# Products of Wv and M by heads, in 32-column tiles of TensorE

## Chip, cores and metric

The kernel runs on one core of a Trainium2 chip. The metric is the device time of one execution in microseconds (us), the median of several runs.

## The reference

A block with adaptive layer norm: linear attention, then a gated feed-forward network, on x of 2048 rows by 1024 columns. Cut to what matters here:

```
mod = silu(c) @ w_mod                       # six rows of 1024: sa, ca, ga, sb, cb, gb
h   = layernorm(x) * (1 + ca) + sa
q, k, v = split(h @ wqkv)                   # 32 heads of 32
pq, pk  = phi(q), phi(k)                    # phi(t) = (t + 1 if t > 0 else exp(t)) + 1e-6
kv  = einsum('bhsd,bhse->bhde', pk, v)      # per head, 32 x 32
z   = sum over s of pk                      # per head, 32
o   = (pq @ kv) / (pq @ z + 1e-6)
x   = x + ga * (o @ wo)
x   = x + gb * ((gelu(h2 @ w_gate) * (h2 @ w_up)) @ w_down),  h2 from layernorm(x), cb, sb
```

The inputs are bf16.

## The kernel before

v itself is never formed. For each group g of four heads (128 columns, `NG` = 8 groups) the kernel computes M = pk^T h, 128 x 1024 (`m_tile`, with a column of ones that gives z), transposes it with a DMA (`m_t`, the tile `MTB`, two buffers used in turn, g % 2), and multiplies it with the group's columns of Wv (`kv_prod`): kv = M Wv, summed over 1024 in 8 steps of 128 (`dc`). In `kv_prod` one matmul per step makes a full 128 x 128 product of all four heads with all four heads; the blocks that belong to one head lie on the diagonal, and VectorE takes out two 64 x 64 pieces, multiplies them by a block mask (`BMASK`) and writes them to `KVT` (L920).

After that `w2_pair(i)` multiplies kv of groups 2i and 2i + 1 with rows of wo (W2 = kv wo, in 64 x 64 tiles of the array, L1203), scaled before by ga (`wofold`, L1214); `den` makes the denominators (L1246) and `mod_rows` the modulation rows (L840), both in 32-column tiles; `wo_mm` multiplies pq with W2 (L1292).

The order on TensorE is written by hand: a loop over 24 tiles (g, k) of `m_tile`, three for each group, and a table `HOOK` that says what follows tile n. Tile n accumulates in PSUM bank n % 4 and ScalarE copies it out (`mcp`, L900). Before the change `kv_prod` always uses bank 4; `w2_pair` uses banks 4 to 7, `den` 3 and 5, the modulation rows behind tile 16 bank 2. Groups 5, 6 and 7 come behind the last tile and between the first `wo_mm`. SP's queue issues the transposes and loads in program order too.

For VectorE, ScalarE and GpSimd the order inside this stretch is not the program's but that of a planner (`Sched.reorder`): it runs through the operations with estimated costs and, whenever an engine is free, takes among the operations that are ready by then the one with the earliest due time. The costs are a table in us per operation, by engine and kind; for TensorE it has

```
"m": (0.145, 0.15), "kv": (0.056, 0.15), "den": (0.027, 0.15), "modr": (0.04, 0.15)
```

and the table applies to each matmul. VectorE's sums over weights of the modulation (L796, L798, L816, L819: `acc`, `gacc`) have no part in the attention and fill its time; the row `gbr` of the table and `modp` read them.

Of the kernel before, what the change touches and what calls it, by code (L numbers as in the profile page):

```python
# [8 lines left out]
ALU = mybir.AluOpType  # L9

P = 128
# [6 lines left out]
NDC = D // P  # L18
NG = 8
HPG = 4  # L20
# [310 lines left out]
def bass_adaLN_cond__linear_attn_block__geglu_ffn__prompt_kernel(  # L331
# [18 lines left out]
    with ExitStack() as es:  # L350
# [3 lines left out]
        ps_all = es.enter_context(nc.psum_tensor("ps_all", [P, 8 * 512], f32))  # L354
        ps16 = ps_all.bitcast(bf16)

        def at(name, shape, dty, off):
            return nc.alloc_sbuf_tensor_at(name, shape, dty, offset=ABASE + off, align_bytes=4)
# [20 lines left out]
        WV = at("wv", [P, NG, NDC, P], bf16, OFF_WK)  # L379
# [12 lines left out]
        MTB = [at(f"mtb{i}", [P, NDC, P], bf16, OFF_MTB[i]) for i in range(2)]  # L392
# [21 lines left out]
        KVT = at("kvt", [P, NG, P], bf16, OFF_KVT)  # L414
# [22 lines left out]
        IDENT, BMASK, BM32, Z32 = (_small[k] for k in ("ident", "bmask", "bm32", "z32"))  # L437
# [7 lines left out]
        def r_sm(name):  # L445
            return [(SMO[name], SMO[name] + SMSZ[name], name)]
# [27 lines left out]
        def r_mtb(i):  # L474
            return [(OFF_MTB[i], OFF_MTB[i] + 2048, f"mtb{i}")]

        def r_wv(g):
            return [(OFF_WK + g * 2048, OFF_WK + (g + 1) * 2048, "wv")]
# [61 lines left out]
        def r_kvt(g0, g1):  # L540
            return [(OFF_KVT + g0 * 256, OFF_KVT + g1 * 256, "kvt")]

        def pr(b):
            return [(b * 2048, (b + 1) * 2048)]

        def PS(b, c0=0, c1=512):
            return ps_all[:, b * 512 + c0: b * 512 + c1]
# [4 lines left out]
        sch = Sched()  # L552
        T, A, V, G, Q = PE_, ACT_, DVE_, POOL_, SP_
# [12 lines left out]
        def pset_writer(b, o):  # L566
            for t_ in pr(b):
                sch.ps.set_writer(t_[0], t_[1], o)
# [49 lines left out]
        for q in range(1, 4):  # L618
            wmq_dma(q)
            for d0, d1 in ((2 * q, 2 * q + 1), (2 * q + 1, 2 * q + 2)):  # L620
# [8 lines left out]
               rd=r_sm("c8") + r_sm("ident"), pwr=pr(4))  # L629
# [4 lines left out]
               rd=r_sm("thc") + r_sm("chalf"), wr=r_sm("siluT"))  # L634
# [173 lines left out]
        def gb_rows():  # L808
            mod_rows(((0, 2, 6, lambda j, h: (HLG[:, j, h, :], r_hlg(j, h))),))
            o_gb[0] = mod_store(2, 6, MRG, [(OFF_TMP + 4096, OFF_TMP + 5120, "mrg")], 2)  # L810
# [94 lines left out]
        def m_t(g):  # L905
            i = g % 2
            tdma(Q, MTB[i][:, :, :], MB[g][:, :], r_mb(g), r_mtb(i), f"mT{g}")

        def kv_prod(g, bank):
            i = g % 2  # L910
            o = None
            for dc in range(NDC):
                o = sch.op(T, lambda e, dc=dc: e.matmul(PS(bank, 0, P), WV[:, g, dc, :], MTB[i][:, dc, :],  # L913
                                                        start=(dc == 0), stop=(dc == NDC - 1)),
                           rd=r_wv(g) + r_mtb(i), pwr=(pr(bank) if dc == 0 else ()), note=f"kv g{g} dc{dc}")
            pset_writer(bank, o)
            z = 64 * (g % 2)
            for h in range(2):
                a, gz = 64 * h, g // 2 * 2 + h
                sch.op(V, lambda e, a=a, gz=gz: e.tensor_tensor(KVT[z:z + 64, gz, 0:64], ps_all[a:a + 64, bank * 512 + a:bank * 512 + a + 64], BMASK[a:a + 64, a:a + 64], ALU.mult),  # L920
                       prd=pr(bank), rd=r_sm("bmask"), wr=r_kvt(gz, gz + 1), note=f"kvt{g}", overwrite_ok=True)

        bank_i = [0, 4]
# [137 lines left out]
        def nbank():  # L1061
            b = ROT[bi[0] % 8]
            bi[0] += 1
            return b
# [6 lines left out]
        def wofold(*kcs):  # L1071
            for kc in kcs:
                rg = r_wo(kc)
                sch.op(V, lambda e, kc=kc: e.tensor_tensor(WO[:, kc, :], WO[:, kc, :], GAB[:, :], ALU.mult),
                       rd=rg + R_GAB, wr=rg, note=f"wofold {kc}")
# [92 lines left out]
        def ga_pass():  # L1168
            b = 6
            mod_rows(((0, 2, b, hl_src),))  # L1170
            o_r = mod_store(2, b, MROW0, [(XHO[2], XHO[2] + 1024, "mrow0")], 0)
            row_load(GAB, R_GAB, 0, 0, "gab", o_r)
# [6 lines left out]
        for n, (kind, a_, b_) in enumerate(seq):  # L1179
            bank = nbank()  # L1180
# [11 lines left out]
        def z32():  # L1192
            sch.op(V, lambda e: e.tensor_tensor(Z32[:], BM32[:], ZCOLS[:, :].unsqueeze(2).to_broadcast([P, NG, NH]), ALU.mult),
                   rd=r_sm("bm32") + r_sm("zcols"), wr=r_sm("z32"), note="z32")
# [32 lines left out]
        def mod_pass():  # L1227
            assert mdone[0] >= 48 and not late
            mod_rows(((2, 4, 2, hl_src),))
            o_sc[0] = mod_store(4, 2, MROW[1], r_2k(OFF_ROW + 2048, "mrow1"), 1)  # L1230
# [3 lines left out]
        def mod_load():  # L1234
            for dst, nt, a0 in ((SBT, "sbT", 0), (CBT, "cbT", 2)):
                sch.dma(Q, lambda e, dst=dst, a0=a0: e.dma_start(dst[:, :], scr_row[1, a0:a0 + 2, :].rearrange("a (b p) -> p (a b)", p=P)),
                        wr=r_sm(nt), deps=[o_sc[0]], note=nt)
# [3 lines left out]
        def den(pr_, b):  # L1241
            o = None
            for g in range(NG):
                for i in range(4):
                    sg, t0 = 2 * pr_ + i // 2, (i % 2) * HW
                    o = sch.op(T, lambda e, g=g, i=i, sg=sg, t0=t0: e.matmul(  # L1246
                        ps_all[32 * i:32 * (i + 1), b * 512:b * 512 + HW], Z32[:, g, :], PQ[sg][:, g, t0:t0 + HW],
                        start=(g == 0), stop=(g == NG - 1)),
                        rd=r_sm("z32") + r_pq(sg, g, g + 1, t0, t0 + HW), pwr=(pr(b) if g == 0 else ()), note=f"den{pr_} {g}.{i}")
            pset_writer(b, o)  # L1250
            sch.op(V, lambda e: e.tensor_scalar(RDC[:, :], PS(b, 0, HW), 1e-6, None, op0=ALU.add), prd=pr(b), wr=r_sm("rdc"), note=f"dene{pr_}")
            sch.op(V, lambda e: e.reciprocal(RDC[:, :], RDC[:, :]), rd=r_sm("rdc"), wr=r_sm("rdc"), note=f"rden{pr_}")
            def store():
                o_rd[pr_] = sch.dma(Q, lambda e: e.dma_start(scr_rd[2 * pr_:2 * pr_ + 2].rearrange("s f k g t -> (s f k g) t"), RDC[:, :]),
                          rd=r_sm("rdc"), note=f"rden{pr_}.st")
            return store
# [30 lines left out]
        def wo_mm(c_, b0, gs):  # L1287
# [9 lines left out]
            if gs[-1] == NG - 1:  # L1297
# [10 lines left out]
        wo_load(1)  # L1308
        NWO = 5
        tiles = [(g, k) for g in range(4) for k in range(3)] + [(g, 0) for g in range(4, NG)] + [(g, k) for g in range(4, NG) for k in (1, 2)]  # L1310
        HOOK = {0: "ga", 6: "kv0", 10: "kv1", 11: "w0", 13: "kv2", 15: "kv3 z32", 16: "modp den0 w1 sbl st0", 17: "rb0.0 rb0.1", 18: "",
                19: "kv4", 20: "den1 gbr st1 ps0.0", 22: "ps0.1"}
        st = {}

        def hook_run(f):
            if f[:2] == "kv":
                kv_prod(int(f[2:]), 4)
            elif f == "ga":
                ga_pass()
            elif f == "gbr":  # L1320
                assert mdone[0] == 64
                gb_rows()
            elif f == "modp":
                mod_pass()
            elif f == "sbl":
                mod_load()
            elif f == "z32":
                z32()
            elif f[:3] == "den":
                st[int(f[3:])] = den(int(f[3:]), (3, 5)[int(f[3:])])  # L1330
            elif f[:2] == "st":
                st[int(f[2:])]()
            elif f[:2] == "ps":
                pq_scale(int(f[2]), int(f[4]), GH[0] + GH[1])
            elif f[:2] == "rb":
                rb_load(int(f[2]), (int(f[4]),))
            elif f[0] == "w":
                w2_pair(int(f[1:]))
# [6 lines left out]
        for n, (g, k) in enumerate(tiles):  # L1345
            m_tile(g, k, n % 4, n % 2)
            if n == len(tiles) - 1:
                kv_prod(5, 4)
            if k == 2:
                m_t(g)  # L1350
            if n == NWO:
                wo_load(2)
                wo_load(3)
            for _ in range(3):
                mod_step()
            if 2 <= n <= 9:
                wofold(n - 2)
            while pend and n > 1:
                wm_dma(*pend.pop(0))
            if n in (6, 7):  # L1360
                gb_load(0, n - 6)
            if n == 11:
                wt_dma(0)
                gb_load(1, 0)
                gb_load(1, 1)
            for f in HOOK.get(n, "").split():
                hook_run(f)
# [487 lines left out]
        for n in range(12):  # L1855
            q, i = divmod(n, 4)
# [6 lines left out]
        for u in range(2 * NFP):  # L1863
# [5 lines left out]
            else:  # L1869
                a = ACTS.get(u, ((), ()))  # L1870
# [143 lines left out]
```

## Time and profile before

| | us |
|---|---|
| median of 3 runs | 781.45 (780.92 to 781.78) |
| the profiled execution | 780.61 |
| its span in the profile | 778.8 |
| TensorE busy | 771.8 (99%) |
| VectorE busy | 649.1 (83%) |
| ScalarE busy | 377.2 (48%) |

The tiles of M and all products of the change lie between about 127 us and 196 us. PE is TensorE's matmuls, PEld its weight loads, DVE VectorE, ACT ScalarE, POOL GpSimd, SP the engine that issues the DMAs; L12 is line 12 of the kernel. Matmuls are pipelined: the time from the start of one to the start of the next is what one costs, and the duration that the profile gives for one is longer. In the chain of waits a row is the start, the length and what was done.

### The profile page before, as it was taken

Reading aid. Unit: us, or ns where it says so; the run is one execution under the profiler, and the core shown is the slowest. Engines: PE = TensorE matmul, PEld = TensorE weight load, DVE = VectorE, ACT = ScalarE, POOL = GpSimd, SP = SyncE. Lnnn points to the kernel's source line nnn. Section 1 sums busy time; section 2 is a strip of 40 time slices with the busy share of each in tenths; the row PEclk is TensorE's granted clock in tenths of the full one; section 3 lists DMA queues with packets and bytes.
Section 4 is the critical chain, followed back from the end, with each engine's and each line's share of the span. In section 5 each row is a group of like instructions: output and inputs, shape, how many; then the busy total and the mean of one; then the engine's idle time right before and its main releaser. Section 6 shows DMA issues by size and latency. Waiting matters only on the chain.

```text
span 778.8 us, 10822 instructions
## 1 busy us (share of the span) xinstructions
PE 771.8 (99%) x3879; PEld 498.5 (64%) x3879; DVE 649.1 (83%) x970; ACT 377.2 (48%) x635; POOL 48.8 (6%) x126
## 2 busy tenths in 40 slices
PE   7999999999999999999999999999999999999998
PEld 4444445666445667767676767677676667777776
DVE  6699989897898878787989888888989987667668
ACT  2497743242484477877755565555555221101111
POOL 2131300000331011100000000000000000000000
PEclk9999999999999999999999999999999999999999
DMA  9789749949996258967353865535356434443341
GB/s 287 254 172 249 160 93 220 258 124 206 209 274 177 82 146 205 234 172 216 100 144 108 256 205 174 145 100 162 92 153 213 138 124 126 136 148 100 130 144 54
DMA packets 196941, 130.22 MB, mean 167 GB/s; under 512 B 69517, under 2 KB 182677, under 8 KB 195865
## 3 DMA queue, kind: packets, MB, share of 16 engines
q1 hardware_dynamic: 196872, 129.55, 61.9%
q8 instruction: 30, 0.49, 0.3%
q14 instruction: 23, 0.18, 0.1%
q10 hardware_dynamic: 16, 0.00, 0.0%
HBM read 92.55 MB, written 23.35 MB: 149 GB/s over the span
## 4 chain that ended last, share of the span: by engine, by line
PE 97%; DMA 1%; SPq 1%; DVE 0%; issue 0%; DVEq 0%
PE ps_all L1472 45%; PE ps_all L1684 22%; PE ps_all L895 7%; PE ps_all L1292 7%; PE ps_all L934 7%; PE ps_all L880 7%; DMA wmq<-in_w_mod_dram 1%; PE ps_all L913 0%; PE ps_all L1607 0%; PE ps_all L766 0%; PE ps_all L1203 0%; PE ps_all L1246 0%; PE ps_all L969 0%; SPq L592 0%; SPq L603 0%; SPq L598 0%
## 5 line engine op out<-in xcount | busy, mean ns | idle before, releaser
L1472 PE MATMUL ps_all<-ss,tp 128*128 128x512 f32 x896 | 214.3, 396 | 0.0
L1472 PEld LDWEIGHTS ps_all<-ss,tp 128*128 128x128 f32 x896 | 168.2, 188 | 37.8 <-DVE ss L1427 0.3
L1684 PE MATMUL ps_all<-dt,sb 128*128 128x512 f32 x440 | 104.7, 394 | 0.0
L1472 PE MATMUL ps_all<-h2a,wt 128*128 128x512 bf16 x448 | 101.5, 380 | 0.0
L1495 ACT ACTIVATE ge<-ps_all 128x512 f32<-128x512 f32 x112 | 64.1, 596 | 73.9 <-DVE ps_all L1483 62.1
L1684 PEld LDWEIGHTS ps_all<-dt,sb 128*128 128x128 f32 x440 | 82.5, 188 | 18.5 <-issue 0.3
L1490 DVE TENSOR_TENSOR ps_all<-ps_all,es 128x512 f32<-128x512 f32 x54 | 37.6, 699 | 49.7 <-ACT es L1480 49.3
L1502 DVE TENSOR_TENSOR ys<-ge,ps_all 128x512 bf16<-128x512 f32 x112 | 74.5, 684 | 2.9
L1472 PEld LDWEIGHTS ps_all<-h2a,wt 128*128 128x128 bf16 x448 | 37.9, 98 | 57.2 <-ACT ps_all L1477 16.9
L1447 DVE TENSOR_TENSOR tp<-wt,tp 128x1024 fp32r<-128x1024 bf16 x56 | 68.2, 1218 | 0.0
L1447 DVE TENSOR_TENSOR tp<-wt 128x1024 fp32r<-128x1024 bf16 x56 | 68.1, 1217 | 0.0
L880 PE MATMUL ps_all<-wk,h1T 128*128 128x512 bf16 x248 | 56.8, 379 | 0.3 <-DVE h1T L724 0.2
L934 PE MATMUL ps_all<-h1T,wq 128*128 128x512 bf16 x256 | 56.7, 379 | 0.0
L1292 PE MATMUL ps_all<-w,pq 128*128 128x512 bf16 x256 | 56.4, 379 | 0.0
L1472 PE MATMUL ps_all<-ar,tp 128*128 128x512 f32 x224 | 55.6, 390 | 0.0
L869 ACT ACTIVATE eb<-ps_all 128x512 f32<-128x512 f32 x64 | 36.4, 593 | 37.0 <-PE ps_all L880 15.2
L1710 ACT ACTIVATE de<-ps_all 128x512 f32<-128x512 f32 x14 | 8.3, 596 | 91.3 <-PE ps_all L1684 91.3
L1684 PE MATMUL ps_all<-wd,ya 128*128 128x512 bf16 x220 | 49.2, 379 | 0.0
L1472 PEld LDWEIGHTS ps_all<-ar,tp 128*128 128x128 f32 x224 | 42.0, 188 | 8.9
L1477 ACT ACTIVATE ps_all<-ps_all 128x512 f32<-128x512 f32 x56 | 32.6, 582 | 30.9 <-PE ps_all L1472 30.9
L934 PEld LDWEIGHTS ps_all<-h1T,wq 128*128 128x128 bf16 x256 | 25.0, 98 | 29.9
L1292 PEld LDWEIGHTS ps_all<-w,pq 128*128 128x128 bf16 x256 | 24.6, 98 | 30.2 <-issue 1.1
(141 smaller groups left out, 985.3 us busy)
## 6 DMA issues: line engine op xcount, KB each, us to landing
wt<-in_B_w_gate_dram SPq DMA_DIRECT2D x28, 512.0 KB, 4.0
wt<-in_B_w_up_dram SPq DMA_DIRECT2D x28, 512.0 KB, 5.2
scr_y<-ys SPq DMA_DIRECT2D x28, 512.0 KB, 3.2
ya<-scr_y SPq DMA_DIRECT2D x14, 896.0 KB, 5.0
rb<-scr_rd SPq DMA_DIRECT2D x32, 256.0 KB, 6.0
wd<-in_B_w_down_dram SPq DMA_DIRECT2D x7, 1024.0 KB, 7.6
wmst<-in_w_mod_dram SPq DMA_DIRECT2D x6, 1024.0 KB, 5.7
wmq<-in_w_mod_dram SPq DMA_DIRECT2D x8, 512.0 KB, 6.7
```

Of the source, the lines that this page charges most:

```text
L869: sch.op(A, lambda e: e.activation(EB[i][:, :], PS(bank), ACTF.Exp), prd=pr(bank), wr=rng, note=f"{note}.exp")
L880: o = sch.op(T, lambda e, dc=dc: e.matmul(PS(bank), H1[sg][:, ci, dc, :], W_[:, dc, jg * 512:(jg + 1) * 512], start=(dc == 0), stop=(dc == ...
L895: o = sch.op(T, lambda e, c_=c_: e.matmul(PS(bank, 0, n), PK[c_][:, g * P:(g + 1) * P], xrow(c_, o_, o_ + n), start=(c_ == 0), stop=(c_ == ...
L934: o = sch.op(T, lambda e, dc=dc: e.matmul(PS(b), WQ[:, dc, qc * P:(qc + 1) * P], H1[sg][:, :, dc, :], start=(dc == 0), stop=(dc == NDC - 1 ...
L1292: last[half] = sch.op(T, lambda e, g=g, half=half: e.matmul(PS(b0 + half), PQ[sg][:, g, ci * P:(ci + 1) * P], W2[:, g, half * 512:(half + ...
L1447: sch.op(V, lambda e: e.tensor_tensor(TP[k][:], in0, in1 if k in (0, 2) else in1[:], ALU.subtract), rd=r0 + r1, wr=r_tp(k), deps=[x1_ops[7 ...
L1472: o = sch.op(T, lambda e, l_=l_, r_=r_, dc=dc: e.matmul(PS(b), l_, r_, start=fresh and dc == 0, stop=dc == ND2 - 1, skip_group_check=True) ...
L1477: sch.op(A, lambda e: e.activation(PS(BB + t), PS(BA + t), ACTF.Copy), prd=pr(BA + t), pwr=pr(BB + t), note="pcp")
L1490: sch.op(V, lambda e: e.tensor_tensor(PS(BC + t), PS(BC + t), ES[t][:, :], ALU.add), prd=pr(BC + t), rd=r_2k(OFF_ES[t], f"es{t}"), pwr=pr( ...
L1495: sch.op(A, lambda e: e.activation(GE[i][:, :], PS(b), ACTF.Gelu_apprx_tanh), prd=pr(b), wr=r_2k(OFF_GE[i], f"ge{i}"), note="gelu")
L1502: sch.op(V, lambda e: e.tensor_tensor(YS[s_][:, 2 * h:2 * h + 2, t, :], q(GE[i][:, :]), q(PS(b + 1)), ALU.mult), rd=r_2k(OFF_GE[i], f"ge{i ...
L1684: o = sch.op(T, lambda e, l_=l_, r_=r_, j=j, dst=dst: e.matmul(dst, l_[:, 0, :], r_, start=(k in (1, 5) or k == 7 and 0 < ca < 4 * CPG - 2 ...
```

## The change

`kv_prod` makes the four 32 x 32 products of the heads alone. Each step of 128 is now four matmuls, one for each head: 32 columns of Wv as weights in one column tile of the array, 32 columns of the transposed M as the moving operand, and the result in 32 partitions and 32 columns of PSUM. So all four heads lie in the same 32 columns, and the eviction reads these twice side by side under the same mask. The planner's table is not changed.

The places change too. Groups 0 and 1 are computed together behind tile 8 (before: behind tiles 6 and 10), groups 2 and 3 together behind tile 15 (before: 13 and 15), group 4 behind tile 20 straight in front of the second denominators (before: behind tile 19). Groups 5, 6 and 7 stay where they are. The banks of groups 0 to 4 are now 3, 4, 1, 2 and 3.

```diff
             for dc in range(NDC):
-                o = sch.op(T, lambda e, dc=dc: e.matmul(PS(bank, 0, P), WV[:, g, dc, :], MTB[i][:, dc, :],
-                                                        start=(dc == 0), stop=(dc == NDC - 1)),
-                           rd=r_wv(g) + r_mtb(i), pwr=(pr(bank) if dc == 0 else ()), note=f"kv g{g} dc{dc}")
+                for h in range(HPG):
+                    o = sch.op(T, lambda e, dc=dc, h=h: e.matmul(ps_all[32 * h:32 * (h + 1), bank * 512:bank * 512 + 32], WV[:, g, dc, 32 * h:32 * (h + 1)],
+                                                                 MTB[i][:, dc, 32 * h:32 * (h + 1)], start=(dc == 0), stop=(dc == NDC - 1)),
+                               rd=r_wv(g) + r_mtb(i), pwr=(pr(bank) if dc == 0 and h == 0 else ()), note=f"kv g{g} dc{dc}.{h}")
...
-                sch.op(V, lambda e, a=a, gz=gz: e.tensor_tensor(KVT[z:z + 64, gz, 0:64], ps_all[a:a + 64, bank * 512 + a:bank * 512 + a + 64], BMASK[a:a + 64, a:a + 64], ALU.mult),
+                sch.op(V, lambda e, a=a, gz=gz: e.tensor_tensor(KVT[z:z + 64, gz, 0:64].rearrange("p (k c) -> p k c", k=2),
+                       ps_all[a:a + 64, bank * 512:bank * 512 + 32].unsqueeze(1).to_broadcast([64, 2, 32]),
+                       BMASK[a:a + 64, a:a + 64].rearrange("p (k c) -> p k c", k=2), ALU.mult),
...
-        HOOK = {0: "ga", 6: "kv0", 10: "kv1", 11: "w0", 13: "kv2", 15: "kv3 z32", 16: "modp den0 w1 sbl st0", 17: "rb0.0 rb0.1", 18: "",
-                19: "kv4", 20: "den1 gbr st1 ps0.0", 22: "ps0.1"}
+        HOOK = {0: "ga", 11: "w0", 15: "kv2 kv3 z32", 16: "modp den0 w1 sbl st0", 17: "rb0.0 rb0.1", 18: "",
+                20: "kv4 den1 gbr st1 ps0.0", 22: "ps0.1"}
...
-                kv_prod(int(f[2:]), 4)
+                kv_prod(int(f[2:]), (1, 4, 1, 2, 3)[int(f[2:])])
...
+            if n == 8:
+                kv_prod(0, 3)
+                kv_prod(1, 4)
```

## The prediction

> **What bounds the kernel now.** I read the page first, then what TensorE waits for, then the chain of waits in order of time over 15 to 30 us and 120 to 200 us, where the edited lines run, then the timeline of the same stretch for the weight loads and VectorE.
>
> ```profile
> PE 771.8 (99%) x3879; PEld 498.5 (64%) x3879; DVE 649.1 (83%) x970; ACT 377.2 (48%) x635; POOL 48.8 (6%) x126
> ...
> PE 97%; DMA 1%; SPq 1%; DVE 0%; issue 0%; DVEq 0%
> ```
>
> TensorE is busy for 99% of the span and makes 97% of the chain that ended last. All its waits:
>
> ```profile
> PE ps_all L628 <- POOL bm L582: 2.5, 1, 2.5
> PE ps_all L766 <- DMA wmq<-in_w_mod_dram: 0.7, 1, 0.7
> PE ps_all L880 <- DVE h1T L724: 0.2, 1, 0.2
> ```
>
> That is 3.4 us, all in the first stages. From 126 us to 196 us it never waits, so every nanosecond that its own instructions lose or gain there moves the end, unless it runs into something that is late. The chain, with the products that change on L913 (x8 is one group, the last x16 two):
>
> ```profile
> 129.34 0.33 PE ps_all L840 x8
> 129.67 14.04 PE ps_all L895 x96
> 143.71 0.45 PE ps_all L913 x8
> 144.16 9.29 PE ps_all L895 x64
> ...
> 171.35 7.08 PE ps_all L895 x48
> ...
> 181.20 0.99 PE ps_all L1246 x32
> 182.19 0.22 PE ps_all L840 x8
> 182.41 7.08 PE ps_all L895 x48
> ...
> 193.62 0.92 PE ps_all L913 x16
> 194.53 0.86 PE ps_all L1292 x4
> 195.40 0.56 PE ps_all L1203 x8
> ```
>
> The reader is to see three prices. A product costs 0.45 us for 8 matmuls, 56 ns each. L840 and L1246 already run in 32-column tiles: two groups of four 256-wide matmuls take 0.22 us behind other such work (182.19), 0.33 us behind full-width work (129.34), so going into tiles costs 0.11 us. Coming back: 48 matmuls of L895 take 7.08 us, where 64 take 9.29 us (145 ns each, 6.97 us for 48), so 0.11 us again.
>
> The narrowest matmuls in the trace, one column against a full weight load:
>
> ```profile
> 23.78 0.38 PE ps_all L766 x16
> ```
>
> 24 ns for a load and its matmul. And loads in 32-column tiles:
>
> ```profile
> 169.31 0.12 PEld L840 LDWEIGHTS ps_all<-hl,ones 128*32 128x32 bf16 x8 [0.28 <-issue]
> ```
>
> Each lasts 92 to 96 ns in the trace's own listing of that line, and all eight are over in 0.12 us: they start within some 25 ns, and in that time four matmuls start between them. So four column tiles load and run beside each other.
>
> **The change, part by part.** Groups are those of four heads, 0 to 7. *Removed:* six times 0.45 us and once 0.92 us (rows of L913 in the chain), 3.62 us of TensorE.
>
> *Added, the products:* each of the 8 becomes 32 loads of 32 columns and 32 matmuls of 32 columns, as 8 groups of four tiles, 64 groups in all. No row shows a group that narrow. Below, streaming alone: the 256-wide group takes 0.11 us, an eighth is 14 ns. Above, the 256-wide group's 109 ns, if the loads and not the columns set it. The nearest row is L766, 24 ns: 32 columns are nearer to 1 than to 256, and the loads run side by side. I take 27 ns, a little more since eight instructions must be issued for it: 64 x 0.027 = 1.73 us.
>
> A rule of the Trainium skill speaks against the change here. Column tiling excludes Fast Weight Load (TensorEngine Tiling (Array Packing), Gotcha 2: Feature Incompatibilities), and a plain load takes its columns over 1.2 in ns (TensorE: Matmul & The Clock Gate, LDWEIGHTS): an estimate of 27 ns for 32 columns. Four in series would make 107 ns a group and the sum +4.1 us; side by side, as the loads of 169.31 start, they change nothing in it.
>
> *Added, the changes of mode:* groups 0 and 1 stand together, 2 and 3 together, 5 alone, 6 and 7 together (they stood so before), each between full-width matmuls: 4 x 0.22 = 0.88 us. Group 4 stands in front of the denominators, which paid for their way in already: nothing.
>
> *VectorE, L920:* the same 16 evictions of 64x64, now reading 32 columns twice. The trace's rows have 210 to 229 ns for one; I take no change. If the repeated read doubled it, only the last four would show: in front of 195.40 they have about 0.1 us to spare (result of group 6 at 194.12, four of 0.25 us, and the product that reads them at 195.40), and groups 6 and 7 coming 0.27 us sooner does not shift that balance, since the four matmuls of L1292 between keep their time. Price at most 0.9 us; below, nothing.
>
> *Moved:* groups 0, 2 and 4 go later and group 1 goes two tiles earlier. Group 1 needs its transposed M: the transpose is issued at 141.96 us and takes 5.6 us to land, 147.6; it is now wanted at about 148.5 us. Margin 0.9 us, cost nothing; if 2 us late it would cost 1.1 us. On SP's queue the transposes into the same two buffers wait for these products: that of g=2 is issued behind tile 8 and needs tile 8's copy anyway (0.46 us after the tile), while group 0 is over 0.3 us after it; those of g=4 and 6 come at least one tile behind their readers. So SP is held no longer. The transposes for groups 4 to 7 land 3.2 to 8.6 us after issue, partly behind the reciprocals' loads (rb), whose start hangs on the denominators and so moves forward with TensorE: group 5 gains on its transpose by 0.24 us, and I cost that at nothing, at most 0.4 us if the transfers do not move.
>
> *PSUM banks:* products used bank 4 only; now group 0 takes bank 3, 2 takes 1, 3 takes 2, 4 takes 3. New waits: tile 11 for group 0's eviction, tile 17 for group 2's, and the modulation rows behind tile 16 (bank 2) for group 3's. The last is tight, and is the second rival below.
>
> *Sum:* -3.62 + 1.73 + 0.88 = -1.01 us. The profiled execution took 780.61 us (span 778.8 and 1.8 around it), so 779.6; the median of the runs is 0.84 us above it: 780.4 us. With both ends of the group's price: -1.84 us at 14 ns, +4.2 us at 109 ns.
>
> **The rivals.**
>
> *Each matmul pays the pace, not each group (slower).* If 24 ns is the least time from one matmul to the next whatever its tile, or the rate at which TensorE is fed, a product costs 32 x 24 = 0.77 us. It decides as soon as a group costs more than 43 ns ((3.62 - 0.88) / 64). Price: 8 x 0.77 + 0.88 - 3.62 = +3.4 us, 784.9 us. For it: the denominators' 32 pairs take 0.87 us, 27 ns each, which does not contradict it, and nothing in the trace issues over some 85 instructions in a microsecond for long, where a product would now need 64 in 0.22 us. Against it: the eight loads in 25 ns. Chance 0.12. The Trainium skill (TensorEngine Tiling (Array Packing), Instruction Overhead) has such an overhead, about 60 cycles for each matmul however narrow, and advises against tiling where a dimension is already small; it does not say whether tiles pay it side by side.
>
> *The order on VectorE.* The kernel's planner writes VectorE's order from a table in which each matmul of a product costs 0.056 us. With 32 instead of 8 it believes a product takes 1.79 us; it will think TensorE some 5 us later behind group 3 than behind the same tile before, and fill VectorE with other work ahead of the evictions. Now:
>
> ```profile
> 168.02 0.48 DVE L920 TENSOR_TENSOR kvt<-ps_all,bmask 64x64 bf16<-64x64 f32 x2
> 168.53 1.23 DVE L1214 TENSOR_TENSOR wo<-wo,gab 128x1024 bf16<-128x1024 bf16 x1
> 171.15 0.42 DVE L1251 TENSOR_SCALAR rdc<-ps_all 128x256 f32<-128x256 f32 x1 [1.39 <-PE ps_all L1203]
> 171.49 0.48 DVE L796 TENSOR_SCALAR gacc<-wmg,silf 128x512 f32<-128x512 bf16 x1
> ```
>
> Group 3's eviction must be over when the rows of L840 want bank 2, at some 168.8 us by my sum; its product is ready at 166.6. If the plan puts the scaling of L1214 (1.2 us) or the first sums of L796 and L798 (0.5 and 0.7 us, on weights whose load is issued at 162.97 us and takes 3.6 to 8.2 us) ahead of it, it ends at 169.6 to 171, and TensorE waits 0.8 to 2.2 us: 781.2 to 782.6 us. Against it: VectorE stood idle for 1.06, 1.47 and 0.24 us in front of earlier evictions, which it can now fill. Chance 0.20, of which 0.05 over +1.56 us.
>
> *Cheaper than I think.* At 14 ns a group, with drains shorter because the tiles are: -1.8 us, 779.6 us. For it: streaming is all that the 256-wide groups show. Against: no pair in the trace takes less than 24 ns. Chance 0.18 for more than 1.56 us.
>
> *It does not do what it says:* tiles that do not run side by side give the first rival's time or the 109 ns end, 785.6 us, and are in its chance.
>
> **How the numbers follow.** 0.2% is 1.56 us, about what a measurement of this kernel can tell from no change. My forecast, 780.4 us, has 0.46 and lies within it; a late transpose or slower evictions (0 to +1 us) have 0.04, the order on VectorE 0.15 within and 0.05 beyond, the pace 0.12, the cheap case 0.18. Faster 0.18, same 0.65, slower 0.17. The range holds forecast and cheap case from 779.4 us, and reaches past VectorE's 2.2 us to 783.0; left out are the pace and some of the tails.
>
> **What would show it.** On the chain: L913 some 0.22 us for x32 and 0.43 us for x64; the first L895 behind each stretch 0.11 us late; group 4 and the denominators in one piece of some 1.2 us. TensorE still without waits after 126 us. Wrong if L913 shows 0.8 us for x32 (the pace), or if PE waits for kvt on L920 or for mtb.

## The result, and the profile after

The changed kernel takes 784.16 us (median of 6 runs, 783.11 to 785.54), the kernel before in the same comparison 781.49 us (6 runs, 780.57 to 781.90). The ratio is 1.0036, with the interval 1.0023 to 1.0049: slower by some 2.7 us, where I had forecast 780.4 us and at most 783.0. The profiled execution took 783.11 us with a span of 781.3 us, 2.5 us more span than before. The edits move the lines behind them: the product of L913 is now L914, the eviction L921, the denominators L1249, W2 L1206, `wo_mm` L1295.

The page of the changed kernel, the busy times and the shares of the chain that ended last:

```profile
PE 768.1 (98%) x4017; PEld 496.9 (64%) x4071; DVE 650.0 (83%) x970; ACT 377.3 (48%) x635; POOL 48.5 (6%) x126
...
PE 88%; DVE 4%; SPq 3%; DMA 3%; issue 1%; ACT 0%; DVEq 0%; ACTq 0%
```

TensorE's busy time is 3.7 us less and the kernel is longer. But most of the 3.7 us is not work saved: this trace has 4017 matmuls against 4071 weight loads, so 54 matmuls have no record. A second profile of the kernel before (experiment 0) lacks 54 as well, and shows almost the same busy time as the changed kernel:

```profile
PE 768.5 (99%) x3825; PEld 498.4 (64%) x3879; DVE 649.2 (83%) x970; ACT 377.3 (48%) x635; POOL 49.4 (6%) x126
```

What the products save is added up below from starts. The chain, 97% TensorE's before, now runs through VectorE, transfers and the queue that issues them for a tenth of its length. So the loss must be in waits, and what TensorE waits for says which (us in total, times, longest):

```profile
PE ps_all L628 <- POOL bmask L581: 2.1, 1, 2.1
PE ps_all L914 <- DMA mtb<-mb: 1.7, 1, 1.7
...
PE ps_all L840 <- DVE kvt L921: 0.6, 1, 0.6
PE ps_all L914 <- DMA scr_rd<-rdc: 0.3, 1, 0.3
```

The first was there before and lies in the first stages. The other three are new and lie in the stretch from 126 to 196 us, where TensorE never waited. They are the three that I had costed at nothing, or left to a rival: group 1's transposed M, group 3's eviction, and group 5's transposed M. (For the last the list names `scr_rd`, a store that is issued behind this transpose, at 186.91 us, and lands with it; group 5's product starts at 191.90 us, the transpose lands at 191.76 us and the store at 192.05 us, so it is the transpose that the product waits for.) A row of 0.2 us "issue" on L1295, left out here, is one of the missing records. The weight loads of the changed kernel show the first of the three new waits, in the stretch of groups 0 and 1:

```profile
148.53 0.27 PEld L914 LDWEIGHTS ps_all<-mtb,wv 128*32 128x32 bf16 x32 [0.28 <-issue]
150.59 0.27 PEld L914 LDWEIGHTS ps_all<-mtb,wv 128*32 128x32 bf16 x32 [1.78 <-DMA mtb<-mb]
```

Group 0's 32 loads go at once, group 1's stand 1.78 us. The chain of the changed kernel, for the products and the other two waits:

```profile
138.97 10.55 DMA wmst<-in_w_mod_dram
...
171.06 0.23 DVE kvt L921
171.31 0.24 DVE kvt L921
171.55 0.04 issue
171.59 0.61 PE ps_all L840 x8
...
173.64 9.40 PE ps_all L895 x64
183.04 0.31 PE ps_all L914 x32
183.34 0.91 PE ps_all L1249 x32
...
186.91 5.00 DMA scr_rd<-rdc
191.91 0.36 PE ps_all L914 x32
...
196.14 0.61 PE ps_all L914 x64
```

A lone product takes 0.31 us with the way back, against 0.45 before; two take 0.61 against 0.92. So the edit does on TensorE what it says. Added up by the starts of TensorE's instructions, from the first L840 (129.27 us before, 129.51 after) to the last long stretch of `wo_mm` (195.88 and 198.36), the stage takes 66.61 us before and 68.85 after: 2.24 us more. Group 1 costs 1.75 of it (2.36 us for the two products, 0.61 without a wait), group 3's eviction 0.65, group 5 0.40: 2.80 us, less what the products save, 0.78 by experiment 3. That is 2.02. Of the 0.22 us left, 0.16 lie in the last product of W2, whose later loads wait for group 7's eviction: L1206 takes 0.72 us there, and 0.56 us before and in experiment 3. The rest lies in the first matmuls of `wo_mm` behind group 5. The other 0.24 us of the span lie ahead of the edited lines.

**Why the transpose was late.** SP's queue before, and then after (start, length, operation):

```profile
113.98 0.37 SPq L595 DMA_DIRECT2D wmst<-in_w_mod_dram  x1
...
136.39 1.21 SPq L595 DMA_DIRECT2D wmst<-in_w_mod_dram  x2
141.96 1.25 SPq L703 DMA_TRANSPOSE mtb<-mb  x1
```

```profile
117.08 0.37 SPq L595 DMA_DIRECT2D wmst<-in_w_mod_dram  x1
...
138.29 1.82 SPq L595 DMA_DIRECT2D wmst<-in_w_mod_dram  x2
142.21 2.98 SPq L703 DMA_TRANSPOSE mtb<-mb  x1
```

Group 1's transpose is issued at nearly the same time, 142.21 against 141.96 us. But it takes 8.3 us to land where it took 5.6. The answers for the tile `mtb` from 120 to 155 us, before and after; group 1's is the shortest in both:

```profile
DMA to landing us min/median/max: 5.6/6.2/6.7
```

```profile
DMA to landing us min/median/max: 8.3/9.6/11.0
```

In front of it stand two loads of modulation weights of 1 MB each, issued 1.9 us later than before, and they land at 145.1 and 149.5 us instead of 142.1 and 145.1: both are still under way when the transpose is issued, and the second for 7.3 us more instead of 3.1 us. They are late because the load of the same kind at 113.98 us is 3.1 us late, and all of SP's queue behind it. That one waits until its buffer has been read, by the sums of L819 on VectorE; of the tile `wmst`, 100 to 122 us, before and then after:

```profile
L819 DVE SCALAR_TENSOR_TENSOR acc<-wmst,silf,acc x7: 743/744/745, 102.2 to 113.1; 128x512 f32<-128x512 bf16 x7
```

```profile
L819 DVE SCALAR_TENSOR_TENSOR acc<-wmst,silf,acc x7: 744/746/748, 102.4 to 116.2; 128x512 f32<-128x512 bf16 x7
```

The last of the seven sums starts at 116.2 us instead of 113.1. Nothing in that stretch is edited; only the order has changed. Before, VectorE's timeline has one such sum behind nearly every operation on k (L870, L872), one each 1.0 to 1.3 us at the end; now it has one for every two of them, one each 1.7 us.

### The profile page after: what moved, and what is told of

Read it like the earlier page. It is cut to its first block, busy times and chain, and to the rows that moved or that the text cites. A ratio compares the mean times of both kernels' runs of the same rounds, so it can differ in the third digit from the quotient of the medians.

```text
span 781.3 us, 11153 instructions
## 1 busy us (share of the span) xinstructions
PE 768.1 (98%) x4017; PEld 496.9 (64%) x4071; DVE 650.0 (83%) x970; ACT 377.3 (48%) x635; POOL 48.5 (6%) x126
## 4 chain that ended last, share of the span: by engine, by line
PE 88%; DVE 4%; SPq 3%; DMA 3%; issue 1%; ACT 0%; DVEq 0%; ACTq 0%
PE ps_all L1478 45%; PE ps_all L1690 22%; PE ps_all L1295 7%; PE ps_all L937 7%; PE ps_all L880 6%; DVE acc L819 2%; SPq L598 2%; DMA wmst<-in_w_mod_dram 1%; PE ps_all L895 1%; SPq L603 1%; DMA scr_rd<-rdc 1%; DMA wk<-in_A_wqkv_dram 1%; DVE acc L798 1%; DVE wo L1217 0%; PE ps_all L1613 0%
## 5 line engine op out<-in xcount | busy, mean ns | idle before, releaser
L1478 PE MATMUL ps_all<-h2a,wt 128*128 128x512 bf16 x421 | 95.4, 379 | 1.9
L1295 PE MATMUL ps_all<-w,pq 128*128 128x512 bf16 x249 | 55.5, 379 | 0.7 <-DVE pq L1284 0.2
L1690 PE MATMUL ps_all<-wd,ya 128*128 128x512 bf16 x211 | 47.4, 379 | 0.6
L1295 PEld LDWEIGHTS ps_all<-w,pq 128*128 128x128 bf16 x256 | 24.6, 98 | 30.4 <-issue 1.1
```

The source lines that it names most:

```text
L1295: last[half] = sch.op(T, lambda e, g=g, half=half: e.matmul(PS(b0 + half), PQ[sg][:, g, ci * P:(ci + 1) * P], W2[:, g, half * 512:(half + ...
L1478: o = sch.op(T, lambda e, l_=l_, r_=r_, dc=dc: e.matmul(PS(b), l_, r_, start=fresh and dc == 0, stop=dc == ND2 - 1, skip_group_check=True) ...
L1690: o = sch.op(T, lambda e, l_=l_, r_=r_, j=j, dst=dst: e.matmul(dst, l_[:, 0, :], r_, start=(k in (1, 5) or k == 7 and 0 < ca < 4 * CPG - 2 ...
```

## The experiments

Kernels that were timed together share the runs of the kernel before, so its time differs by some tenths from one group of experiments to the next. In experiments 0, 3, 10, 11 and 12 lines are shifted by one to three. "Stage" is the time from the first L840 to the last long stretch of `wo_mm`; a few profiles lack a matmul's record at its end, which is worth 0.2 us and is allowed for.

**1. The planner is told the true price.** On the changed kernel:

```diff
-"kv": (0.056, 0.15)
+"kv": (0.00625, 0.15)
```

> The changed kernel, with one entry of the planner's table mended: a matmul of a product costs 0.00625 us, so that a product of 32 costs it the measured 0.20 us and not 1.79 us. Theory A (the planner's false price of a product writes the order on VectorE that holds SP's queue and delays group 1's transposed M and group 3's eviction): the waits of 1.7 and 0.6 us go, and it takes about 780.5 us, 1.0 under the kernel before. Theory B (the new places are to blame, since they change the planner's due times and ask for group 1 two tiles sooner, whatever a product is said to cost): it stays 2 to 3 us above the kernel before, and the weights of the modulation (L595) are again issued at about 117 us and not 114 us. Theory C (tiles and mode changes themselves cost more than they bring): also 2 to 3 us above.

Measured: 783.56 us against 781.18, ratio 1.0031 (1.0019 to 1.0042). What TensorE waits for in it:

```profile
PE ps_all L914 <- DMA mtb<-mb: 2.6, 2, 1.4
```

The wait for group 3's eviction is gone (tile 16 takes 2.42 us again), so it came from the false price. But the early load is still late (issued at 116.58 us), group 1's transpose lands at 150.22 us and costs 1.4 us, and group 5's costs 1.2 instead of 0.4. The false price brought a wait of 0.65 us and not the body of the loss; by the clock this version (1.0031) and the changed kernel (1.0036) can't be told apart.

**2. The false price alone.** The kernel before, with `"kv"` at 0.224 for each of its 8 matmuls, so that the planner believes in 1.79 us a product:

> The kernel before, unchanged on TensorE and SP; only the table says 0.224 us for each of the 8 matmuls of a product, so that the planner believes 1.79 us for it, as it does in the changed kernel. The prediction's second rival as it was put (a false price alone rewrites VectorE's order so that evictions come late and TensorE waits): 1 us or more slower, 782.2 us or more, with waits on kvt. Theory B (the price does little by itself where nothing is asked for sooner): within 0.7 us of before, no wait on the transposed M.

Measured: 781.33 against 781.11, 1.0001 (0.9992 to 1.0010); TensorE waits for nothing between 126 and 196 us. The wrong price does change the order on VectorE, but the early load is issued at 114.35 us, hardly later than the 113.98 us of before. With the old places there is slack for the wrong price; it does harm only together with the new ones.

**3. The changed kernel with the order of before.** The planner's result for VectorE, ScalarE and GpSimd is replaced by before's order as a list; only the evictions of groups 0 to 3 stand where their products now come.

```diff
-        sch.reorder(mark[0], mark[1], (DVE_, ACT_, POOL_), {id(x4_op): 8.0})
+        for e_ in (DVE_, ACT_, POOL_):
+            ...  # the operations of the stretch, sorted by the list ORDER[e_]
```

> The changed kernel with the planner switched off: VectorE, ScalarE and GpSimd run in the order that the planner wrote for the kernel before, only that the evictions of groups 0 and 1 stand behind the sum that ends at about 149 us, and those of 2 and 3 behind the mask product of z. TensorE and SP keep the changed kernel's order. Theories A and B for the order (either way VectorE's order is what delays SP and the transpose): L595 is issued at 114 us, group 1's transposed M lands at about 147.6 us and nothing waits for it; 780.4 to 781 us. The place alone (group 1 wanted too soon under any order): still 1 to 2 us of wait on the transposed M, 782 us or more. Theory C: 783 to 784 us.

Measured: 781.05 against 781.18, 0.9998 (0.9989 to 1.0007). The chain (the product is L917 here):

```profile
149.01 0.61 PE ps_all L917 x64
149.62 7.07 PE ps_all L898 x48
...
181.05 0.31 PE ps_all L917 x32
...
193.68 0.61 PE ps_all L917 x64
```

The early load goes out at 114.63 us, group 1's transpose lands at 149.16 us, just in time, and none of the three waits is there. It takes 6.5 us to land here, so the margin of 0.9 us is gone even without a wait. The stage is 0.78 us shorter than before. The whole loss was in the order on the other engines. The gain doesn't show in the median, whose interval (-0.9 to +0.5 us) holds both 0.78 us and nothing.

**4. Tiles alone.** Old places, bank 4, and a price of 0.014, with which the orders on all other engines are those of before:

```diff
-        HOOK = {0: "ga", 11: "w0", 15: "kv2 kv3 z32", ...
+        HOOK = {0: "ga", 6: "kv0", 10: "kv1", 11: "w0", 13: "kv2", 15: "kv3 z32", ...
...
-            if n == 8:
-                kv_prod(0, 3)
-                kv_prod(1, 4)
```

> Only the column tiles: the products stay at the places and in the bank that they had before, and the table says 0.014 us for a matmul, so that a product costs the planner the same 0.448 us and the other engines keep the order of before exactly. Seven stretches (groups 0 to 5 alone, 6 and 7 together) pay 0.22 us each for the change of mode, 1.54 us, or one less if group 4 lay beside the denominators, which it doesn't here; the products bring 8 times 0.25 us. Theories A and B: 0.4 to 0.5 us faster than the kernel before, 781.0 us, without waits of TensorE. Theory C: slower by 2 us or more.

Measured: 781.02 against 781.18, 1.0001 (0.9992 to 1.0010). The chain:

```profile
143.59 0.30 PE ps_all L914 x32
143.89 9.39 PE ps_all L895 x64
153.28 0.31 PE ps_all L914 x32
```

0.30 us and 0.10 us on the following stretch (9.39, before 9.29), against 0.45 us: 0.04 to 0.05 us saved for a lone product, 0.21 for two together. The stage is 0.41 us shorter. So the tiles without the new places do no harm, and bring too little to be seen in the median.

**5. Places alone.** Full-width products of 8 matmuls at their right price, in the new places and banks:

```diff
-                kv_prod(int(f[2:]), 4)
+                kv_prod(int(f[2:]), (1, 4, 1, 2, 3)[int(f[2:])])
...  # and HOOK and the two calls behind tile 8 as in the change
```

> Only the new places and banks: the products are full-width matmuls as before, at 0.056 us each in the table, which is right for them. Theory A (false price): as the kernel before, within 0.5 us, since the price is right. Theory B (places and the due times that follow from them): 2 to 3.5 us slower, with a wait of 1 to 2 us for group 1's transposed M. Theory C: as the kernel before.

Measured: 783.13 against 781.18, 1.0024 (1.0016 to 1.0033); the early load goes out at 116.56 us and TensorE waits 1.6 us for group 1's transpose. No tile and no false price is in it: the places bring 1.95 us of loss, where the whole change lost 2.7.

**9. Groups 0 and 1 alone.** The kernel before, with nothing changed but these two products:

```diff
-        HOOK = {0: "ga", 6: "kv0", 10: "kv1", 11: "w0", ...
+        HOOK = {0: "ga", 11: "w0", ...
...
+            if n == 8:
+                kv_prod(0, 3)
+                kv_prod(1, 4)
```

> The kernel before, full-width products at their old price in the table; only groups 0 and 1 move behind tile 8, in banks 3 and 4. Theory B1 (asking for group 1 two tiles sooner makes every tile up to the sixth due sooner in the plan, so VectorE puts the evictions of q and k ahead of the sums over the modulation weights, the buffer of L595 comes free 3 us later, SP's queue behind it is late, and the transposed M with it): L595 at about 116.6 us, a wait of 1 to 2 us on the transposed M, and 1.5 to 2.5 us slower than before, 782.7 to 783.7 us. Theory B2 (the loss needs the later moves and banks too): within 0.7 us of before.

Measured: 783.09 against 781.11, 1.0026 (1.0017 to 1.0035). The wait and its place in the chain:

```profile
PE ps_all L913 <- DMA mtb<-mb: 2.2, 1, 2.2
```

```profile
142.44 9.02 DMA mtb<-mb
151.46 0.05 issue
151.50 0.62 PE ps_all L913 x8
```

One move of two products loses 2.0 us, as much as all the new places together. The early load is late here too, issued at 116.85 us.

**11. The same with the order of before.** Experiment 9, with the list of experiment 3 (evictions of groups 0 and 1 at their new place):

> The kernel in which only groups 0 and 1 moved, full-width, that lost 2 us, now with the order of before on VectorE, ScalarE and GpSimd (evictions of groups 0 and 1 behind the sum that ends at about 149 us). If the order that the planner writes for the sooner group 1 is the cause: L595 at 114 us, the transposed M for group 1 lands with no more than 0.3 us of wait, 781.1 us, as before. If the sooner place itself is the cause: a wait of 1 us or more stays, 782.2 us or more.

Measured: 781.53 against 781.53, 1.0000 (0.9991 to 1.0009). SP's queue:

```profile
114.59 0.37 SPq L598 DMA_DIRECT2D wmst<-in_w_mod_dram  x1
...
142.57 1.25 SPq L706 DMA_TRANSPOSE mtb<-mb  x1
```

And of the tile `mtb`, 120 to 155 us, group 1's again the shortest:

```profile
DMA to landing us min/median/max: 5.9/6.6/7.4
```

Issued 0.13 us later than in experiment 9, the transpose lands 3 us earlier, at 148.46 us, and TensorE does not wait. Same products, same places, another order on VectorE, ScalarE and GpSimd. So it isn't the place that costs; it is the order that the planner writes for it.

**12. Half of two loads.** The changed kernel, where the two loads ahead of group 1's transpose carry half of their rows:

```diff
+            h = 4 if t in (8, 9) else NDC
-            return sch.dma(Q, lambda e: e.dma_start(WMST[sl][:], wm_v[:, :, t * 512:(t + 1) * 512]), ...
+            return sch.dma(Q, lambda e: e.dma_start(WMST[sl][:, 0:h, :], wm_v[:, 0:h, t * 512:(t + 1) * 512]), ...
```

> The changed kernel, order and places as they are, but the two loads of modulation weights that are under way when group 1's transpose is issued (L595 at 138.3 and 139.0 us) bring half the rows, 0.5 MB each instead of 1 MB; the sums over the other half read what the buffer held before, so the second modulation row is not the reference's. If the transpose lands late because these transfers share the DMA engines with it: it lands 2 us or more sooner, the wait for group 1 goes, and the kernel is 1 to 2 us faster than the changed one, 782 to 783 us. If SP's lateness or the transpose itself is the cause: it still lands at 150 us and the wait of 1.7 us stays.

Measured: 782.22 against 781.53, 1.0011 (1.0003 to 1.0020). The early load is as late as ever (117.47 us) and the transpose is issued at 142.59 us, later than in the changed kernel; yet of the tile `mtb`, 120 to 155 us:

```profile
DMA to landing us min/median/max: 5.6/6.4/7.1
```

5.6 us again, landed at 148.16 us, and no wait for it. That closes the chain: the transpose was slow because two 1 MB loads were still under way. What is left, but for some tenths, is the other wait, which is now larger:

```profile
PE ps_all L841 <- DVE kvt L922: 1.4, 1, 1.4
```

In the changed kernel TensorE came to this point late already, and most of the lateness of group 3's eviction was hidden behind that; take the first wait away and 1.4 us appear where 0.6 were. The waits of one stage can't be added as if each stood alone.

**6. A later place.** The changed kernel with the true price, groups 0 and 1 behind tile 10 and group 2's transpose behind them, group 3 in bank 4:

```diff
-            if n == 8:
+            if n == 10:
                 kv_prod(0, 3)
                 kv_prod(1, 4)
-            if k == 2:
+                m_t(2)
+            if k == 2 and n != 8:
                 m_t(g)
```

> The changed kernel with groups 0 and 1 together behind tile 10 instead of tile 8 (the transpose of group 2, which writes over group 0's buffer, follows them), group 3 in bank 4 and the true price of 0.00625 us in the table. If what hurts is that group 1 is wanted too soon: no wait for the transposed M of group 1, 0.8 us less than before, 780.4 us. If VectorE's order stays bad because the planner has less time of TensorE to fill: L595 at 116 us or later and waits for later transposes, 782 us or more.

Measured: 782.72 against 781.11, 1.0022 (1.0014 to 1.0031). Group 1's transpose is in time, but the planner defers the sums as before (early load at 116.90 us), and TensorE waits 1.2 us for group 5's transpose, 0.4 for a copy of VectorE's (`hlg`) and 0.3 for an eviction.

**7. A mixture.** Groups 0, 1 and 5 full width in their old places, 2 and 3 together in tiles, 4 in front of the denominators, 6 and 7 in tiles, with a price for each kind:

```diff
+"kt": (0.00625, 0.15)
...
+            o, full = None, g in (0, 1, 5)
...
-                kv_prod(int(f[2:]), (1, 4, 1, 2, 3)[int(f[2:])])
+                kv_prod(int(f[2:]), (4, 4, 1, 4, 3)[int(f[2:])])
```

> Column tiles only where they pay and nothing is asked for sooner: groups 0, 1 and 5 stay full-width at their old places, 2 and 3 stand together behind tile 15 (group 3 in bank 4, so that no modulation row waits for its eviction), 4 in front of the denominators, 6 and 7 together; the table has 0.00625 us for a matmul of a tiled product. By the measured prices (two products together 0.61 us and 0.09 us for the way in against 0.89 us, one beside the denominators 0.22 us against 0.45 us): 0.19 + 0.23 + 0.19 = 0.6 us less, 780.6 us, no wait of TensorE after 126 us. Theory C (tiles cost more than they bring): slower than before.

Measured: 782.22 against 781.11, 1.0013 (1.0004 to 1.0022). TensorE's new waits, the first that for group 5:

```profile
PE ps_all L914 <- DMA scr_rd<-rdc: 0.7, 1, 0.7
...
PE ps_all L840 <- DVE hlg L804: 0.4, 1, 0.4
```

By the starts they are 0.9 and 0.7 us, more than the 0.6 that the tiles save.

**10. The mixture with the order of before.**

> A version meant to beat both: groups 0, 1 and 5 full-width at their old places, 2 and 3 in tiles behind tile 15 (group 3 in bank 4), 4 in tiles in front of the denominators, 6 and 7 in tiles together, and the order of before on the other engines, with the evictions of group 2 beside those of group 3. If the planner's order made the mixed version lose: TensorE waits for nothing behind 126 us, and by the measured prices it takes 0.6 us less than before, 780.6 us. If the tiles' gain is lost to something behind them (reciprocals' loads, the modulation rows): 781 to 782 us, with TensorE waiting for group 5's transposed M.

Measured: 782.10 against 781.53, 1.0008 (0.9999 to 1.0017). The wait for `hlg` is gone; that for group 5 is not:

```profile
184.83 5.78 DMA scr_rd<-rdc
190.61 0.59 PE ps_all L917 x8
```

(The row names the store `scr_rd` again; it is issued behind the transpose and lands at 190.74 us, when the product has started.) Group 5's transpose lands at 190.46 us, where before had it at 188.68 with some half a microsecond to spare. In the queue it stands behind a store of reciprocals and eight loads (`rb`). These are not what is late: the last of them lands at 188.05 us against 187.80 before, and the transpose is issued at 180.36 us against 180.11. But it lands 2.4 us behind that load and not 0.9. In between, from 188.3 to 189.5 us, the DMA engines move next to nothing (0 to 10 GB/s). The kernel before has such a pause too, but behind the landing. What the pause is, and why it falls where it does, stays open.

**0. The kernel before with its own order as a list,** instruction for instruction the same program:

> The kernel before once more, instruction for instruction on every engine (the planner's order is written out as a list instead of being computed). Every theory: no difference. What the comparison shows is the size of a difference that means nothing here, expected under 0.2 us in the medians, and a second profile of the same program shows how far the times of the first 126 us and of the stretch behind 196 us move by themselves.

Measured: 781.48 against 781.53, 1.0002 (0.9993 to 1.0011). So a tenth of a percent says nothing here, and experiments 2, 3, 4, 10 and 11 stay "no difference" by the clock. No version was faster than the kernel before beyond its interval.

## Why the prediction was wrong

**The step that failed** is under *Moved*: "Margin 0.9 us, cost nothing; if 2 us late it would cost 1.1 us". I took the landing of group 1's transposed M from the trace of before and held it against the new wish. It landed 2.9 us later, at 150.5 us, and cost 1.75 us. The transfer was not issued later; its neighbours were. I had asked what SP's queue would be held by behind the products, and not whether anything ahead of them would move. With a planner that orders three engines by due times, a product asked for two tiles sooner changes the order from the eviction of k on, 30 us ahead of the edit: sums over modulation weights are put back, a buffer is free 3 us later, a load goes out 3 us later, and the two loads ahead of the transpose land up to 4.4 us later. Experiments 9 and 11 show that this order is the cause, 12 that the loads are the means. Which due time in the planner's list tips it is my reading of its rule, and was not tried.

**The second rival, the order on VectorE**, had the right mechanism in the main and was too small a part of the forecast. It named bank 2, group 3's eviction, and L1214 or the first sums of L796 and L798 ahead of it. VectorE's timeline after:

```profile
166.69 1.22 DVE L1217 TENSOR_TENSOR wo<-wo,gab 128x1024 bf16<-128x1024 bf16 x1
167.82 0.75 DVE L798 SCALAR_TENSOR_TENSOR acc<-wmg,silf,acc 128x512 f32<-128x512 bf16 x1
168.49 0.42 DVE L1196 TENSOR_TENSOR z<-bm,zcols 128x256 bf16<-128x256 bf16 x1
168.82 0.75 DVE L798 SCALAR_TENSOR_TENSOR acc<-wmg,silf,acc 128x512 f32<-128x512 bf16 x1
169.60 0.47 DVE L921 TENSOR_TENSOR kvt<-ps_all,bmask 64x64 bf16<-64x64 f32 x2
170.34 0.69 DVE L804 TENSOR_TENSOR hlg<-acc,hlg 128x512 bf16<-128x512 f32 x1 [0.26 <-ACT hlg L803]
171.06 0.48 DVE L921 TENSOR_TENSOR kvt<-ps_all,bmask 64x64 bf16<-64x64 f32 x2
```

Group 2's two evictions at 169.60 and group 3's at 171.06 us, with the scaling of L1217 ahead of them, as the rival had it. The sums that it named are not there (L796 comes behind, at 171.57 us); the two of L798 are of another row (`acc`, not `gacc`), and stood ahead of group 3's eviction before, too. What it did not name is L804, which waits for ScalarE and lies between the two groups' evictions: 1.0 us with its wait. The last eviction ends at 171.5 us, past the end of the range that I gave (169.6 to 171). TensorE waited 0.65 us in the changed kernel, and 1.4 us where nothing had delayed it before (experiment 12): the rival's 0.8 to 2.2 us. That the price does it alone fell with experiment 2; that it takes part was shown by experiment 1.

**Group 5's transpose**, "at most 0.4 us", cost 0.40 us in the changed kernel, but 1.2 in experiments 1 and 6 and 0.9 to 1.3 in 7 and 10. The bound was made for a gain of 0.24 us on TensorE alone. In these five versions the transpose lands at 190.5 to 191.8 us and not at 188.7; the changed kernel waits least since it comes there latest. In experiment 10, which has the order of before, the transpose is issued hardly later and only lands later, so the order is not all of it; the rest is not explained.

**What held.** The product's price: groups of four start 25 ns apart in the trace (I took 27), so the rival of a pace of 24 ns per matmul is out, as is the cheap case of 14 ns. The Trainium skill's overhead of about 60 cycles for each matmul (TensorEngine Tiling (Array Packing), Instruction Overhead) can hold in these runs only if four tiles pay it side by side: the four of such a group start 1 to 5 ns apart. The way in and out of the tiles: 0.09 and 0.10 us where I took 0.11 each. Evictions: 0.47 and 0.48 us for two, as before, so the repeated read is free. Transposes of groups 2 and 4 held SP no longer. The sum on TensorE: -0.78 us in experiment 3 against -1.01; a stretch of two costs 0.71 us with both ways, not 0.65, which is 0.18 us over three stretches. The evictions in front of the last W2 product are in time in experiments 3 and 4, where it takes 0.56 us as before; only the changed kernel and experiment 12 lose 0.16 us there.

## What to carry to other kernels

Where a planner or a list sets the order of other engines, a moved step changes work far ahead of it: compare the orders of all engines from before and after the edit, first of all the readers that free buffers for loads, before any margin is read from the old trace. A transfer's landing time is not its own: hold against a margin what would be under way with it if the queue ran some microseconds later. And when several waits lie in one stage, take them away one at a time; each hides part of the next.

## What the runs showed of the hardware that I had not expected

The transposing DMA of a 128 x 1024 bf16 tile landed 5.6 us after its issue where the second of the two 1 MB loads ahead of it landed 3.1 us after that issue, and also where the loads were halved to 0.5 MB each (some 3 us). It landed 8.0 to 9.0 us after its issue where that load landed 6.5 to 7.4 us after it (the changed kernel, experiments 1, 5 and 9). The landing follows the load's: in all fourteen profiles it comes behind it, by 2.5 to 2.6 us in ten and by 1.0 us in four. So the margin could have been read from the load and not from the time since the issue. What makes it 2.5 or 1.0 us is open.

In a stretch of two products the first one's groups of four start 25 ns apart. The second one's matmuls start evenly, 8.3 ns apart, 33 ns for four (experiment 3 and the changed kernel alike): 4.2 ns for each of the 8 instructions of a group. So 32 pairs of load and matmul go at the price of the groups, 64 don't quite: 0.61 us with the way back, where twice the lone product's 0.22 us and the way would be 0.53. That it is the feeding of instructions which runs out behind the first 32 is an inference from the step. The changed kernel fits it: behind the wait of 1.75 us for its transposed M, group 1's groups start 25 ns apart again. A stretch of three products would tell more, and was not run.
